# A linear-attention block in one kernel: layernorm applies put ahead of k's exponentials, their statistics a pass sooner, the last v/S tile on two engines

## The chip, the core and the metric

The kernel runs on one core of a Trainium2 chip. The core has TensorE (matrix products, results in PSUM), VectorE, ScalarE (activation functions), GpSimd and SyncE, which here only issues DMAs. In the profile they are PE (and PEld for its weight loads), DVE, ACT, POOL and SP. Each engine works through its own queue in order and waits on semaphores for the others. The metric is the device time of one execution in microseconds (us): a median of 277.12 us in three runs (277.02 to 277.51).

## The reference, cut to what matters

```python
def _A_ref(x, wqkv, w_phi, wo):
    qkv = (x @ wqkv).reshape(B, S, 3, H, Dh)...            # S=2048, D=640, H=32, Dh=20
    q, k, v = qkv[0], qkv[1], qkv[2]
    pq, pk = q @ w_phi, k @ w_phi                          # per head, 20x20
    phi_q = concat([softmax(pq), softmax(-pq)])            # over the 20 features of a head
    phi_k = concat([softmax(pk), softmax(-pk)])
    kv = einsum("bhsf,bhsd->bhfd", phi_k, v)
    z  = einsum("bhsf->bhf", phi_k)
    o = (phi_q @ kv) / (phi_q @ z + 1e-6)
    return o.reshape(B, S, D) @ wo

h  = x + _A_ref(layernorm(x), ...)
h2 = h + (gelu(layernorm(h) @ w_gate) * (layernorm(h) @ w_up)) @ w_down   # F = 1536
```

The softmax of k and its negative gives two "signs", 0 and 1, each with its own sum S over the 20 features of a head. The kernel does not divide the exponentials by S; it divides v by it, which gives the same kv.

## The kernel before, in words

The 2048 rows are 16 tiles of 128 rows. The whole kernel is recorded in a manual schedule: on every engine the instructions run in the order in which the source issues them, and only semaphores hold them.

A first phase makes the layernorms of tiles 0 to 5 and the folded k weights. Then the loop `for t in range(NT)` (L443) runs 16 passes. Pass t does, in source order:

- `k_tile(t)` (L300): TensorE's k product (10 matmuls of 128x320) into a PSUM tile pk, then on ScalarE two exponentials (L305, plus and minus) into E, the numerators of both signs.
- in pass 0 `ln_ap(6)`, made on VectorE; in passes 10 to 14 `fold`, which makes a part of the folded q weights; in pass 15 four q products and their exponentials.
- `kv_tile(i)` (L332) for the tiles that KVG names: the product of E and vt, 20 matmuls for each tile, sign 0 first; tiles 0 and 1 in pass 5, 2 to 5 in pass 9, 6 to 9 in pass 13, the rest at the end.
- in passes 1 to 11 `v_mm(t + 4)`: the v product of a tile four ahead; it reads LN1T, the transposed layernorm of that tile.
- in passes 1 to 9 `ln_ap(t + 6, on_act=True)` (L256): ScalarE writes the layernorm ln of a tile six ahead (L133), from rstd and mr; SP then issues a DMA that transposes it into LN1T (L149).
- `v_ev(t + 4)` (L291): ScalarE copies v from PSUM to vS.
- in even passes up to 6 `ln_st(t + 8, t + 9)` (L252): the layernorm statistics of two tiles. VectorE makes bn_stats and bn_aggr (L109, L113), GpSimd makes ve, rstd and two mr (L121, L122, L127).
- `k_norm(t)` (L308): VectorE sums E (the reduce sk, L312) and takes reciprocals (rs, L316). Then the v/S products (L320): sign 1 of every tile on GpSimd; sign 0 on GpSimd for the tiles in VP, otherwise on VectorE, put off until after the next tile's reduce. Tile 15's sign 0 product follows its reciprocal at once.

In pass 10 VectorE also makes the layernorms of tiles 0 and 1, which the q products of pass 15 read once SP's transposes have landed. SP's queue holds, in this order, the layernorm transposes, loads of the q weights in passes 7 to 10, the transposes of tiles 0 and 1, and in pass 13 the loads of Wg, Wo and Wu.

PSUM tiles of the loop come from a ring (`gtile`): four buffers up to pass 2, three from pass 3 on, where the fourth becomes the accumulator kvp of the kv products. So a k or v product waits until ScalarE has read the tile three allocations earlier.

After the loop, `kv_mask` (L342) brings kvp into the matrix KV, and the rest of the kernel (attention, output projection, the two layers of the feed-forward part) follows from 71 us on.

Of the kernel before, what the change touches and what calls it, by code (L numbers as in the profile page):

```python
# [10 lines left out]
ALU = mybir.AluOpType  # L11
# [6 lines left out]
def kernel(  # L18
# [12 lines left out]
    nc = tc.nc  # L31
    P = 128
    S = 2048
    D = 640
    H = 32
    Dh = 20
    FF = 1536
    NT = S // P
# [5 lines left out]

    H0 = [(P * c) // Dh for c in range(NC)]
    NH = [(P * c + P - 1) // Dh - H0[c] + 1 for c in range(NC)]
    VP = (0, 2, 4, 6, 9, 11)
    KA, QA = (0, 2, 4), (0, 1, 2, 3, 4)
    LQ = (7, 8, 9, 9, 10)
    FQ = (10, 11, 12, 13, 14)  # L50
# [6 lines left out]
    VC = Dh + 1  # L57
# [3 lines left out]
    UH = H // 2  # L61
# [34 lines left out]
    def small(pool, shape, name, bufs=3):  # L96
        return pool.tile(shape, F32, name=name, bufs=bufs)

    def gtile(name):
        return psG.tile([P, 2, 512], F32, name=name, tag="G")  # L100

    def ln_stats(pool, tiles, tag, act=True, between=None, log=False):

        n = len(tiles)
        mv = small(pool, [P, n, nc.vector.BN_AGGR_DIM], "mv" + tag)
        stats = small(pool, [P, n, 2, nc.vector.BN_STATS_DIM], "stats" + tag)
        for j, xt in enumerate(tiles):
            for i in range(2):
                nc.vector.bn_stats(stats[:, j, i, :], xt[:, i * HD:(i + 1) * HD])  # L109
                if between and i == j == 0:  # L110
                    between()
        for j in range(n):
            nc.vector.bn_aggr(mv[:, j, :], stats[:, j])  # L113
        ve = small(pool, [P, n], "ve" + tag)
        rstd = small(pool, [P, n], "rstd" + tag)
        if log:

            nc.scalar.activation(ve, mv[:, :, 1], ACTF.Ln, bias=eps)
            nc.scalar.activation(rstd, ve, ACTF.Exp, scale=-0.5)
        else:  # L120
            nc.gpsimd.tensor_scalar_add(ve, mv[:, :, 1], EPS)  # L121
            nc.gpsimd.tensor_tensor(rstd, ve, nhalf[:, 0:n], op=ALU.pow)  # L122

        mr = small(pool, [P, n], "mr" + tag)
        if act:
            for j in range(n):
                nc.gpsimd.tensor_scalar(mr[:, j:j + 1], mv[:, j, 0:1], rstd[:, j:j + 1], -1.0,  # L127
                                        op0=ALU.mult, op1=ALU.mult)
        return [(xt, mv[:, j, 0:1], rstd[:, j:j + 1], mr[:, j:j + 1]) for j, xt in enumerate(tiles)]
# [11 lines left out]
    def transpose_to(dst, src, on_pe, on_dve=False):  # L141

        if on_pe:
            tp = psG.tile([P, 16, P], BF16, name="tp", tag="G")
            for c in range(NC):
                nc.tensor.transpose(tp[:, c, :], src[:, c * P:(c + 1) * P], ident)
            (nc.vector.tensor_copy if on_dve else nc.scalar.copy)(dst, tp[:, 0:NC, :])  # L147
        else:
            nc.sync.dma_start_transpose(dst, src)  # L149
# [12 lines left out]
    vS = [p1.tile([P, H, VC], BF16, name=f"vS{i}") for i in range(8)]  # L162
# [89 lines left out]
    def ln_st(*tiles, act=True, between=None, log=False):  # L252
        for t, v in zip(tiles, ln_stats(p1, [x_sb[t // 4][:, t % 4, :] for t in tiles], "1", act, between, log)):
            lnp[t] = v

    def ln_ap(t, on_act=False, on_pe=False):  # L256
        ln = (ln_act if on_act else ln_dve)(p1, "1", *lnp[t])
        if on_pe:
            lnp[t] = ln
        else:  # L260
            transpose_to(LN1T[t // 4][:, :, t % 4 * P:(t % 4 + 1) * P], ln, False)
# [8 lines left out]
    def proj(ps, t, W, us=(0, 1), rows=False):  # L270
        for u, c in sorted(((u, c) for u in us for c in range(NC)), key=lambda x: x[::-1] if rows else x):
            nc.tensor.matmul(ps[:, u, 0:HD], lhsT=lnT(t, c), rhs=W[:, c, u * HD:(u + 1) * HD],  # L272
                             start=(c == 0), stop=(c == NC - 1))
# [26 lines left out]
    def k_tile(t):  # L300
        pk = gtile("pk")
        proj(pk, t, Wk2, rows=t == 0)
        Ek[t] = ev.tile([P, 2, D], BF16, name="E", bufs=8)
        for s in range(2):
            nc.scalar.activation(Ek[t][:, s, :].rearrange("p (u f) -> p u f", u=2), pk[:, :, 0:HD],  # L305
                                 ACTF.Exp, scale=((lnp[t][2], nrstd[t]) if t in CT else (1.0, -1.0))[s])

    def k_norm(t):  # L308


        sk = small(p1, [P, 2 * H], "sk")
        nc.vector.reduce_sum(sk, Ek[t].rearrange("p s (h f) -> p (s h) f", f=Dh), axis=AX.X)  # L312
        if t - 1 in todo:
            todo.pop(t - 1)()
        rs = small(p1, [P, 2 * H], "rs")
        nc.vector.reciprocal(rs, sk)  # L316
        Vt[t] = vt = ev.tile([P, 2, H, VC], BF16, name="vt", bufs=8)

        def mult(s, eng):
            eng.tensor_tensor(vt[:, s], vS[t % 8], rs[:, s * H:(s + 1) * H, None].to_broadcast([P, H, VC]), ALU.mult)  # L320

        mult(1, nc.gpsimd)
        if t in VP:
            mult(0, nc.gpsimd)
        elif t == NT - 1:
            mult(0, nc.vector)
        else:
            todo[t] = lambda: mult(0, nc.vector)

# [2 lines left out]
    def kv_tile(t):  # L332

        for s in range(2):
            for c in range(NC):
                for u in range(2):
                    f0, h0 = u * HD + c * 64, u * UH + 3 * c
                    nc.tensor.matmul(kvp[HALF[u], s, c * 4 * VC:(c + 1) * 4 * VC],  # L338
                                     lhsT=Ek[t][:, s, f0:f0 + 64], rhs=Vt[t][:, s, h0:h0 + 4, :],
                                     start=(c == 0 and t == 0), stop=(t == NT - 1), skip_group_check=True)  # L340
# [13 lines left out]
    def q_mm(j, part=(0, 1)):  # L354

        if 0 in part:
            pqs[j] = gtile("pq")
        for i, bc in enumerate(QG[j]):
            if i not in part:
                continue  # L360
            b, c = divmod(bc, NC)
            for kc in range(NC):
                nc.tensor.matmul(pqs[j][:, i, :], lhsT=Wq2[:, kc, c * P:(c + 1) * P], rhs=LN1T[b][:, kc, :],  # L363
                                 start=(kc == 0), stop=(kc == NC - 1))

    def q_exp(j, signs=(0, 1)):
        for s in signs:
            nc.scalar.activation(Eq[j][:, :, s, :], pqs[j][:, 0:len(QG[j])], ACTF.Exp, scale=(1.0, -1.0)[s])  # L368
# [74 lines left out]
    for t in range(NT):  # L443
        if t == T3:
            ps_cm.close()
            psG = ps_cm.enter_context(tc.tile_pool(name="psG", bufs=3, space=PSUM, reuse_waits="tile"))
            psK = ps_cm.enter_context(tc.tile_pool(name="psK", bufs=1, space=PSUM, reuse_waits="tile"))
            kvp = psK.tile([P, 2, 512], F32, name="kvp")
        k_tile(t)
        if t == 0:  # L450
            ln_ap(6)
        if t in FQ:
            fold(WqT, Wq2, True, [i for i, f in enumerate(FQ) if f == t])
        for j in range(len(QT)):
            if t == QT[j]:
                q_mm(j)
                q_exp(j)
        for i in KVG.get(t, ()):
            kv_tile(i)
        if 0 < t < NT - 4:  # L460
            v_mm(t + 4)
        if t > 0 and t + 6 < NT:
            ln_ap(t + 6, on_act=True)
        if 0 < t < NT - 4:
            v_ev(t + 4)
        if t % 2 == 0 and t + 8 < NT:
            ln_st(t + 8, t + 9)
        k_norm(t)
        load_T(WqT, 0, *[i for i, f in enumerate(LQ) if f == t])
        if t == 10:  # L470

            for i in CT:
                ln_ap(i)
        if t == 9:
            nc.gpsimd.memset(KV, 0.0)
            nc.gpsimd.memset(kmask, 1.0)
            for r in HALF:
                nc.gpsimd.affine_select(out=kmask[r], in_=kmask[r], pattern=[[4, NC], [-Dh, 4]],
                                        compare_op=ALU.is_ge, fill=0.0, base=0, channel_multiplier=1)
                nc.gpsimd.affine_select(out=kmask[r], in_=kmask[r], pattern=[[-4, NC], [Dh, 4]],  # L480
                                        compare_op=ALU.is_ge, fill=0.0, base=Dh - 1, channel_multiplier=-1)
            nc.gpsimd.tensor_copy(KV[:, :, 0, :, KC - 1], kmask)
            nc.gpsimd.tensor_copy(KV[:, :, 1, :, 0], kmask)
        if t == 13:
            nc.sync.dma_start(Wg, wg_v)
            nc.sync.dma_start(Wo, wo_v)
            nc.sync.dma_start(Wu, wu_v)
# [338 lines left out]
```

## Time and profile before

| what | value |
|---|---|
| median of 3 runs | 277.12 us (277.02 to 277.51) |
| the profiled execution, its time | 278.27 us |
| its span, first to last instruction | 276.4 us |
| mean granted TensorE clock | 1.000 |
| busy: PE, DVE, ACT, POOL | 271.0, 176.8, 139.2, 97.2 us |
| DVE busy from 20 to 65 us | 4.90 to 5.00 of every 5 us |
| POOL product (L320, 128x672) | 22 times, 1.34 us each |
| DVE product (L320, 128x672) | 10 times, 0.85 to 1.71 us |

A timeline line gives the start and the duration in us from the span's start, the engine, the source line, the operation with its output and inputs, the count of merged instructions, and in brackets the idle time ahead of it with what ended it. Where several instructions are merged the duration reaches from the start of the first to the end of the last. In the list of waits, a line reads: engine and line that waited, engine and line that ended the wait, us in total, how often, the longest. Buffer numbers are left out of the names, so vt is any tile's v/S.

### The profile page before, as it was taken

How to read it: one execution, taken by the hardware profiler on the slowest of the kernel's cores; microseconds unless marked ns; L12 is line 12 of the kernel's file. 1: busy time of each engine (PE TensorE's matmuls, PEld its weight loads, DVE VectorE, ACT ScalarE, POOL GpSimd, SP SyncE). 2: the span in 40 equal slices, each digit the busy share in tenths (PEclk: the TensorE clock that was granted, in tenths of full speed). 3: DMA queues.
4: the chain of work that ended last, by engine and by line, in shares of the span. 5: the costliest groups of instructions: out<-in, count | busy, mean ns of one | idle time of the engine just before them, and what ended most of it. 6: DMA issues, size and time to landing. Idle time of an engine off the chain costs nothing.

```text
span 276.4 us, 5943 instructions
## 1 busy us (share of the span) xinstructions
PE 271.0 (98%) x2348; PEld 173.5 (63%) x2348; DVE 176.8 (64%) x335; ACT 139.2 (50%) x239; POOL 97.2 (35%) x218
## 2 busy tenths in 40 slices
PE   8999999999999999999999999999999999999995
PEld 4676767775455887788764555675555577444574
DVE  6889999999496776576477773346876333322322
ACT  4879897878489856365543255223245410223100
POOL 4238897774302316355303553102165400000000
PEclk9999999999999999999999999999999999999999
DMA  7963436489730021414111133110123111000011
GB/s 208 191 225 71 53 67 102 71 242 392 271 122 0 4 47 26 95 29 97 24 50 47 26 58 62 25 67 9 47 47 71 26 47 50 25 0 0 2 47 47
DMA packets 42235, 21.37 MB, mean 77 GB/s; under 512 B 35040, under 2 KB 40416, under 8 KB 42208
## 3 DMA queue, kind: packets, MB, share of 16 engines
q1 hardware_dynamic: 42208, 21.01, 30.1%
q8 instruction: 18, 0.29, 0.5%
q14 instruction: 9, 0.07, 0.1%
HBM read 10.18 MB, written 2.62 MB: 46 GB/s over the span
## 4 chain that ended last, share of the span: by engine, by line
PE 79%; DMA 5%; SPq 4%; issue 4%; DVE 3%; POOL 1%; ACT 1%; POOLq 0%; DVEq 0%
PE gu L664 38%; PE pd L683 19%; PE po L604 8%; PE pq L363 5%; PE pv L272 3%; PE ab L532 3%; SPq L186 3%; DMA LN1T<-ln 2%; DMA x_sb<-in_A_x_dram 2%; PE pk L272 2%; DMA WqT<-in_A_wqkv_dram 1%; DVE sk L312 1%; PE kvp L338 1%; DVE rs L316 1%; POOL vt L320 1%
## 5 line engine op out<-in xcount | busy, mean ns | idle before, releaser
L667 ACT ACTIVATE g<-gu 128x512 bf16<-128x512 f32 (+1 forms) x60 | 30.7, 512 | 68.6 <-PE gu L664 68.4
L670 DVE TENSOR_TENSOR GT<-gu,g 128x512 bf16<-128x512 f32 (+1 forms) x60 | 34.4, 580 | 47.9 <-PE gu L664 39.3
L664 PE MATMUL gu<-LN2T,Wg 128*128 128x512 bf16 (+1 forms) x300 | 61.8, 337 | 0.0
L664 PE MATMUL gu<-LN2T,Wu 128*128 128x512 bf16 (+1 forms) x300 | 61.8, 336 | 0.0
L683 PE MATMUL pd<-Wd,GT 128*128 128x320 bf16 (+2 forms) x396 | 53.5, 295 | 0.0
L683 PEld LDWEIGHTS <-GT 128*128 128x128 bf16 x396 | 37.9, 98 | 14.7 <-DVE GT L670 0.2
L664 PEld LDWEIGHTS <-Wu 128*128 128x128 bf16 x300 | 29.3, 98 | 22.6
L664 PEld LDWEIGHTS <-Wg 128*128 128x128 bf16 x300 | 28.8, 98 | 21.4
L272 PEld LDWEIGHTS <-LN1T 128*128 128x128 bf16 x290 | 27.7, 98 | 11.4 <-DMA LN1T<-ln 1.2
L686 DVE TENSOR_TENSOR y<-pd,x_sb 128x320 bf16<-128x320 f32 (+2 forms) x29 | 13.9, 480 | 29.0 <-PE pd L683 29.0
L320 POOL TENSOR_TENSOR vt<-vS,rs 128x672 bf16<-128x672 bf16 x22 | 29.1, 1344 | 9.1 <-DVE rs L316 7.4
L604 PE MATMUL po<-Wo,oT 128*128 128x320 bf16 x160 | 24.3, 299 | 0.0
L272 PE MATMUL pk<-Wk,LN1T 128*128 128x320 bf16 x160 | 24.2, 299 | 0.0
L363 PE MATMUL pq<-LN1T,Wq 128*128 128x512 bf16 x100 | 23.1, 379 | 0.0
L312 DVE TENSOR_REDUCE sk<-E 128x64 f32<-128x1280 bf16 x16 | 22.9, 1429 | 0.0
L368 ACT ACTIVATE Eq<-pq 128x1024 bf16<-128x1024 f32 (+1 forms) x26 | 20.0, 829 | 1.7 <-PE pq L363 1.7
L272 PE MATMUL pv<-Wv,LN1T 128*128 128x320 bf16 x130 | 19.8, 299 | 0.5 <-DMA LN1T<-ln 0.4
L604 PEld LDWEIGHTS <-oT 128*128 128x128 bf16 x160 | 15.6, 98 | 7.4 <-ACT oT L147 0.5
L305 ACT ACTIVATE E<-pk 128x640 bf16<-128x640 f32 x28 | 18.2, 705 | 3.9 <-PE pk L272 3.8
L581 DVE TENSOR_TENSOR tt<-AB,w 128x1280 bf16<-128x1280 f32 x12 | 17.9, 1488 | 1.1 <-POOL w L574 0.9
L133 ACT ACTIVATE ln<-x_sb,v,rstd 128x640 bf16<-128x640 bf16 x14 | 12.9, 920 | 10.7 <-POOL v L643 10.3
L363 PEld LDWEIGHTS <-Wq 128*128 128x128 bf16 x100 | 9.4, 98 | 10.0
(110 smaller groups left out, 292.9 us busy)
## 6 DMA issues: line engine op xcount, KB each, us to landing
out_dram<-y SPq DMA_DIRECT2D x15, 160.0 KB, 1.8
Wg<-in_B_w_gate_dram SPq DMA_DIRECT2D x1, 1920.0 KB, 7.7
Wu<-in_B_w_up_dram SPq DMA_DIRECT2D x1, 1920.0 KB, 13.6
Wd<-in_B_w_down_dram SPq DMA_DIRECT2D x1, 1920.0 KB, 7.8
x_sb<-in_A_x_dram SPq DMA_DIRECT2D x2, 640.0 KB, 7.0
Wo<-in_A_wo_dram SPq DMA_DIRECT2D x1, 800.0 KB, 9.3
x_sb<-in_A_x_dram SPq DMA_DIRECT2D x4, 160.0 KB, 3.2
Wv<-in_A_wqkv_dram SPq DMA_DIRECT2D x2, 320.0 KB, 4.2
```

The source lines that it names most:

```text
L272: nc.tensor.matmul(ps[:, u, 0:HD], lhsT=lnT(t, c), rhs=W[:, c, u * HD:(u + 1) * HD], start=(c == 0), stop=(c == NC - 1))
L305: nc.scalar.activation(Ek[t][:, s, :].rearrange("p (u f) -> p u f", u=2), pk[:, :, 0:HD], ACTF.Exp, scale=((lnp[t][2], nrstd[t]) if t in C ...
L312: nc.vector.reduce_sum(sk, Ek[t].rearrange("p s (h f) -> p (s h) f", f=Dh), axis=AX.X)
L320: eng.tensor_tensor(vt[:, s], vS[t % 8], rs[:, s * H:(s + 1) * H, None].to_broadcast([P, H, VC]), ALU.mult)
L363: nc.tensor.matmul(pqs[j][:, i, :], lhsT=Wq2[:, kc, c * P:(c + 1) * P], rhs=LN1T[b][:, kc, :], start=(kc == 0), stop=(kc == NC - 1))
L368: nc.scalar.activation(Eq[j][:, :, s, :], pqs[j][:, 0:len(QG[j])], ACTF.Exp, scale=(1.0, -1.0)[s])
L581: nc.vector.tensor_tensor(tt.rearrange("p s (h f) -> p s h f", f=Dh), num, w[:, :, :, None].to_broadcast([P, 2, H, Dh]), ALU.mult)
L604: nc.tensor.matmul(pos[u], lhsT=st[t][:, c, :], rhs=Wo[:, c, u * HD:(u + 1) * HD], start=(c == 0), stop=(c == NC - 1))
L664: nc.tensor.matmul(gu[i][:, 0:n], lhsT=W[:, c, f * P:(f + 1) * P], rhs=LN2T[b][:, c, a0:a1], start=(c == 0), stop=(c == NC - 1))
L667: nc.scalar.activation(g[:, 0:n], gu[0][:, 0:n], ACTF.Gelu_apprx_tanh)
L670: nc.vector.tensor_tensor(st[b, "g", f][:, a0:a1], gu[1][:, 0:n], g[:, 0:n], ALU.mult)
L683: nc.tensor.matmul(ps, lhsT=st[b, "g", f][:, tl * P:(tl + 1) * P], rhs=Wd[:, f, f0:f1], start=(f == 0), stop=(f == NF - 1))
```

## The change

Three edits in the loop, and one in `k_norm`:

- From pass 2 on, the layernorm apply of tile t+6 stands ahead of `k_tile(t)`, so ahead of k's exponentials on ScalarE; in pass 1 it stays where it was.
- The statistics of tiles 10 to 15, in pairs, move from passes 2, 4 and 6 to passes 1, 3 and 5.
- Tile 13's sign 0 product goes to GpSimd (VP gets 13).
- Tile 15's sign 1 product is cut by heads: the first 16 on GpSimd, the other 16 on VectorE, behind VectorE's sign 0 product.

TensorE's and SP's instructions keep their order.

```diff
-    VP = (0, 2, 4, 6, 9, 11)
+    VP = (0, 2, 4, 6, 9, 11, 13)
...
-        def mult(s, eng):
-            eng.tensor_tensor(vt[:, s], vS[t % 8], rs[:, s * H:(s + 1) * H, None].to_broadcast([P, H, VC]), ALU.mult)
-
-        mult(1, nc.gpsimd)
+        def mult(s, eng, a=0, b=H):
+            eng.tensor_tensor(vt[:, s, a:b], vS[t % 8][:, a:b],
+                              rs[:, s * H + a:s * H + b, None].to_broadcast([P, b - a, VC]), ALU.mult)
+
+        mult(1, nc.gpsimd, 0, UH if t == NT - 1 else H)
         if t in VP:
             mult(0, nc.gpsimd)
         elif t == NT - 1:
             mult(0, nc.vector)
+            mult(1, nc.vector, UH)
         else:
             todo[t] = lambda: mult(0, nc.vector)
...
+        if t > 1 and t + 6 < NT:
+            ln_ap(t + 6, on_act=True)
         k_tile(t)
...
-        if t > 0 and t + 6 < NT:
-            ln_ap(t + 6, on_act=True)
+        if t == 1:
+            ln_ap(7, on_act=True)
         if 0 < t < NT - 4:
             v_ev(t + 4)
-        if t % 2 == 0 and t + 8 < NT:
-            ln_st(t + 8, t + 9)
+        if t == 0 or t % 2 and t + 9 < NT:
+            ln_st(t + 9 - (t == 0), t + 10 - (t == 0))
         k_norm(t)
```

## The prediction

> **What bounds the kernel now.** I read the page first (engine table and the sums of the chain), then what TensorE waited for, then the timelines of TensorE, VectorE and GpSimd between 20 and 72 us, the only stretch that the change touches.
>
> ```profile
> span 276.4 us, 5943 instructions
> PE 271.0 (98%) x2348; PEld 173.5 (63%) x2348; DVE 176.8 (64%) x335; ACT 139.2 (50%) x239; POOL 97.2 (35%) x218
> ...
> PE 79%; DMA 5%; SPq 4%; issue 4%; DVE 3%; POOL 1%; ACT 1%; POOLq 0%; DVEq 0%
> ```
>
> TensorE is busy 98% of the span, so the change can only win what TensorE waits for, but can lose whatever it makes TensorE wait. The waits:
>
> ```profile
> PE kvp L338 <- POOL vt L320: 0.5, 1, 0.5
> ...
> PE pv L272 <- DMA LN1T<-ln: 0.4, 1, 0.4
> ```
>
> The first is the last v/S tile (70.17 to 70.72). The second lies at 22.24, on tile 6, whose path is not changed. A third shows only as a gap in TensorE's timeline: by its 1.36 us step the v product of tile 12 should start at 39.91 and starts at 40.20, and the chain leads there through a late layernorm of tile 12. So 0.55 + 0.29 = 0.84 us is the most there is to win.
>
> ```profile
> 38.55 1.52 PE L272 MATMUL pk<-Wk,LN1T 128*128 128x320 bf16 x10
> 40.20 1.53 PE L272 MATMUL pv<-Wv,LN1T 128*128 128x320 bf16 x10
> ...
> 60.24 7.72 PE L363 MATMUL pq<-LN1T,Wq 128*128 128x512 bf16 x35
> 67.89 2.29 PE L338 MATMUL kvp<-vt,E 128*64 128x84 bf16 x110
> 70.72 0.38 PE L338 MATMUL kvp<-vt,E 128*64 128x84 bf16 x10 [0.55 <-POOL vt L320]
> 71.04 2.33 PE L363 MATMUL pq<-LN1T,Wq 128*128 128x512 bf16 x10
> ```
>
> The engine behind these waits is VectorE. In the windows from 20 to 65 us it is busy 4.90 to 5.00 of every 5 us: any time added to its queue there stays in it until the last v/S tile. The layernorms of tiles 0 and 1, which it makes in pass 10, also gate q: the second transpose is issued at 55.56 and, the slower of the two, takes 4.2 us to land (2.6/3.4/4.2 min/median/max), so at 59.8, 0.4 us before q starts at 60.24. That is all the slack it has.
>
> Now how VectorE and GpSimd meet:
>
> ```profile
> 25.13 2.59 POOL L320 TENSOR_TENSOR vt<-vS,rs 128x672 bf16<-128x672 bf16 x2
> 27.81 0.23 POOL L121 TENSOR_SCALAR ve<-mv 128x2 f32<-128x2 f32 x1
> 28.12 0.71 POOL L122 TENSOR_TENSOR rstd<-ve,nhalf 128x2 f32<-128x2 f32 x1
> 28.93 0.96 POOL L127 TENSOR_SCALAR mr<-mv,rstd 128x1 f32<-128x1 f32 x2
> ...
> 27.32 1.43 DVE L312 TENSOR_REDUCE sk<-E 128x64 f32<-128x1280 bf16 x1
> 28.67 0.85 DVE L320 TENSOR_TENSOR vt<-vS,rs 128x672 bf16<-128x672 bf16 x1
> 29.44 0.55 DVE L316 RECIPROCAL rs<-sk 128x64 f32<-128x64 f32 x1
> ...
> 44.03 2.59 POOL L320 TENSOR_TENSOR vt<-vS,rs 128x672 bf16<-128x672 bf16 x2
> ...
> 45.94 1.40 DVE L320 TENSOR_TENSOR vt<-vS,rs 128x672 bf16<-128x672 bf16 x1
> ```
>
> At 28.67 VectorE's product of tile 1 (sign 0) meets only GpSimd's small statistics and takes 0.85. At 45.94 the same instruction finds a GpSimd product running until 46.62 and ends at 47.34, 0.72 after it: it was held. The one at 55.86 takes 1.71 against a GpSimd product that started 0.32 earlier (55.54) and ended at 56.85: again the end plus 0.72. Whoever starts first keeps the other out, and a lead of 0.32 us is enough. In the last pair VectorE starts 0.07 first (68.64 against 68.71), and GpSimd's product takes 1.97 for 1.31.
>
> **The change, part by part.**
>
> *Statistics a pass sooner.* The pairs (10,11), (12,13) and (14,15) move from behind the even reduce to ahead of the odd one. VectorE's work is the same; what moves is the GpSimd queue. There the four statistics instructions now stand between the two products of an even tile and the one of the odd tile. Before, they stood behind it, exactly where VectorE's own product of the odd tile fell. Now the odd tile's GpSimd product falls there:
>
> Tile 1: GpSimd's second product ends at 25.13 + 1.31 = 26.45. The statistics took 27.72 to 29.89 = 2.17, of which the mr pair was held 0.46 (0.96 against 0.50 at 22.98), so 1.71. Product from 26.45 + 1.71 + 0.09 = 28.25 to 29.56. VectorE reaches its product at 28.67 as before (the same work stands ahead of it, in another order). GpSimd leads by 0.42, so VectorE ends at 29.56 + 0.72 = 30.28 for 29.52: +0.75.
>
> Tile 3: the reciprocal of tile 2 now starts at 30.20. GpSimd: 30.75 + 0.22 to start + 2.59 + 1.80 = 35.35, ends 36.66. VectorE: 2.23 (reciprocal and statistics) + 1.53 + 0.47 + 1.35 later, 35.78. Held to 37.38 for 36.63: +0.75.
>
> Tile 5, by the same steps: GpSimd 42.39 to 43.70, VectorE at 42.88, held to 44.42 for 43.73: +0.69.
>
> Sum: VectorE is 2.2 us late from pass 6 on. Bounds of each hold: 0 (VectorE first; then the GpSimd product waits 0.7, which has slack) and 1.3 (a whole product). I take the worked 0.7 because the lead (0.4) lies above the 0.32 that the trace shows to decide.
>
> The Trainium skill ("SBUF — State Buffer", section "SBUF: two separate sides") speaks against such a meeting: the two engines share a port pair under an exclusive lock, and the loser waits out the whole instruction. The rows differ in detail: 0.72 of the 0.85 is still to do after a hold, and the product at 28.67 was not held by the small rstd running until 28.83. By the page's rule taken to the letter, each hold costs 0.13 more, 0.4 in sum.
>
> *Applies ahead of k's exponentials.* Nothing is added; ScalarE makes ln(t+6) 0.92 sooner and E(t) as much later. E is needed by the reduce, which runs at least 1.5 us behind (48.90 to 50.38 in pass 10, over 2 us in passes 2 to 9), and by the PSUM ring of three: v of tile 7 may wait 0.1 for E of tile 2. ln(14) now stands ahead of E of tile 8 and waits for its mr at about 42.1; E of tile 8 then ends near 44.3, not 41.4, and its reduce (now 46.8) still waits for nothing. The copy of v of tile t+8 writes the vS that the held products read, so it now also waits for them: tile 11's, at about 38.7 on ScalarE, needs tile 3's product (37.4), tile 13's, at 46, needs tile 5's (44.4); both are in time. The transposes keep their order on SP. ln(12) gets its mr before 35.0, not at 35.8, so its transpose lands at about 39.2 and the 0.29 at 39.91 goes. But the products of tiles 2 to 5 (from 42.7, twenty matmuls in 0.41) reach tile 5 at 43.97 and wait for 44.42: -0.29 + 0.51 on TensorE.
>
> *What is late next.* The layernorms of tiles 0 and 1 come 2.2 us later, the second lands at 59.81 + 2.2 = 62.0, and SP's Wg, Wo, Wu behind it slide as much (Wo is first read at 80.27, landed by 69). q starts at 62.05 for 60.24: +1.81. TensorE, there at about 60.5, hides its own 0.2 in this wait.
>
> *Tile 13 to GpSimd, last tile shared.* Tile 13's sign 0 product leaves VectorE (0.91) and costs GpSimd 1.31. Reciprocal 13 at 64.90. GpSimd: tile 13 both signs 65.6 to 68.2, tile 14 to 69.45. VectorE: reduce 14 at 65.37, reduce 15 at 67.37, product 14 at 68.72, held to 70.17. So the 0.91 comes back as a hold. Last reciprocal 70.09 to 70.64; VectorE's sign 0 to 71.59; GpSimd's half (half of the 1.17 that it took after VectorE's end: 0.59) to 72.18; VectorE's half after it (half of 0.72) to 72.5. q follows 0.37 after the tile as before: 72.9 for 71.04, +1.85. If VectorE takes its half first, GpSimd's ends at 72.6.
>
> The skill ("GPSIMD Engine Reference", "Engine selection") advises VectorE for elementwise work, GpSimd being about 2x slower on two inputs; the rows say 1.31 to 0.85, 1.5x. By 2x, tile 14 would end 0.4 later and so would the sum.
>
> **Sum.** Both gates agree: q +1.81, last tile +1.85. Behind 71 us TensorE has no slack to give back (50.0 of 50 us busy from 90 to 140), so +1.85 reaches the end. The profiled execution took 278.27 (span 276.4), 1.15 above the median of 277.12; I carry the difference to the median: 278.97, so 279.0, +0.67%.
>
> **Rivals.**
> - *No holds* (VectorE takes the port first, or the GpSimd statistics run 0.4 slower): it decides where GpSimd's lead falls under zero; the rows leave 0.07 to 0.32 open. The 0.29 is won; at the end GpSimd's tile 13 (64.70 to 65.97) and 14 (to 67.24) hold VectorE's product 14 to 67.96 for 68.07, and the shared last tile ends at 70.3 for 70.67: -0.37, 276.75. At most all 0.84: 276.3. For it: 0.1 us of semaphore time would eat a quarter of the lead. Against: the lead is 0.42, 0.43 and 0.49 in the three places.
> - *Some holds only*: one leaves 59.81 + 0.75, q +0.37 and the last tile -0.37 + 0.75: 277.5. Two: +1.1, 278.2.
> - *More than worked*: the second transpose already takes 4.2 for the first's 2.6, with the weights' traffic on its heels; if GpSimd or a landing costs another 1 us there, 280.0.
> - *Hidden*: VectorE late, but TensorE not. Against: 0.4 us of slack at q, none at the last tile.
>
> **Chances.** Forecast 0.66 (its own range 278.4 to 279.6), no holds 0.14, some 0.11, more 0.09. The measurement tells about 0.2% (0.55 us) from no change. Slower: 0.66 + 0.09 + 0.08 of the some = 0.83. Same: 0.03 of the some and 0.08 of no holds = 0.11. Faster: 0.06. The range drops most of "no holds" and the worst of "more": 277.2 to 279.9.
>
> **What would show it.** VectorE's sign 0 products of tiles 1, 3 and 5 at about 1.6 us instead of 0.85; the reciprocal of tile 6 near 44.3; a TensorE wait at the first q for LN1T of about 1.5 us; the gap ahead of tile 12's v product gone; tile 14's product on VectorE held behind GpSimd. I am wrong if those products stay at 0.85.

## The result, and the profile after

The change makes the kernel slower: 278.51 us median (278.08 to 279.31, 6 runs) for 277.38 (277.02 to 277.51), a ratio of 1.0041 with a 95% interval of 1.0029 to 1.0053. Beside the last experiments, on another chip, it was measured again: 1.0037 (1.0023 to 1.0050). So +1.0 to +1.1 us, where +1.85 was forecast. The profiled execution of the changed kernel took 278.30 us, span 276.6.

First the page of the changed kernel, the engine line and the chain that ended last:

```profile
PE 270.0 (98%) x2335; PEld 173.4 (63%) x2348; DVE 179.2 (65%) x335; ACT 138.6 (50%) x239; POOL 96.3 (35%) x219
...
PE 72%; DVE 17%; issue 6%; DMA 1%; ACT 1%; POOL 1%; SPq 0%; DVEq 0%; ACTq 0%
```

VectorE has 2.4 us more of busy time (179.2 for 176.8), although a product of 0.91 us left it and only half a product came to it. Its share of the chain went from 3% to 17% (7% in the later profile of the change, for 4% in that of before): the loop's end now hangs more on its queue. Where it was held, in the timelines of GpSimd, VectorE and TensorE of the changed kernel:

```profile
22.73 2.58 POOL L320 TENSOR_TENSOR vt<-vS,rs 128x672 bf16<-128x672 bf16 x2 [0.38 <-ACT vS L292]
25.41 0.23 POOL L121 TENSOR_SCALAR ve<-mv 128x2 f32<-128x2 f32 x1
25.72 0.71 POOL L122 TENSOR_TENSOR rstd<-ve,nhalf 128x2 f32<-128x2 f32 x1
26.53 0.50 POOL L127 TENSOR_SCALAR mr<-mv,rstd 128x1 f32<-128x1 f32 x2
26.98 1.31 POOL L320 TENSOR_TENSOR vt<-vS,rs 128x672 bf16<-128x672 bf16 x1
...
33.93 1.31 POOL L320 TENSOR_TENSOR vt<-vS,rs 128x672 bf16<-128x672 bf16 x1
...
40.74 1.31 POOL L320 TENSOR_TENSOR vt<-vS,rs 128x672 bf16<-128x672 bf16 x1
...
69.14 1.40 POOL L320 TENSOR_TENSOR vt<-vS,rs 128x336 bf16<-128x336 bf16 x1 [1.35 <-DVE rs L316]
...
26.20 1.43 DVE L312 TENSOR_REDUCE sk<-E 128x64 f32<-128x1280 bf16 x1
27.55 1.47 DVE L320 TENSOR_TENSOR vt<-vS,rs 128x672 bf16<-128x672 bf16 x1
...
34.51 1.45 DVE L320 TENSOR_TENSOR vt<-vS,rs 128x672 bf16<-128x672 bf16 x1
...
41.46 1.31 DVE L320 TENSOR_TENSOR vt<-vS,rs 128x672 bf16<-128x672 bf16 x1
...
67.05 1.46 DVE L320 TENSOR_TENSOR vt<-vS,rs 128x672 bf16<-128x672 bf16 x1
...
69.07 1.83 DVE L320 TENSOR_TENSOR vt<-vS,rs 128x672 bf16<-128x672 bf16 x2
...
60.20 7.71 PE L365 MATMUL pq<-LN1T,Wq 128*128 128x512 bf16 x34 [0.56 <-DMA LN1T<-ln]
...
70.59 0.20 PE L340 MATMUL kvp<-vt,E 128*64 128x84 bf16 x1 [0.22 <-POOL vt L320]
70.95 0.35 PE L340 MATMUL kvp<-vt,E 128*64 128x84 bf16 x9 [0.17 <-DVE vt L320]
```

VectorE's products of tiles 1, 3 and 5 take 1.47, 1.45 and 1.31 us; before, each took 0.85. The first starts at 27.55 while GpSimd's product runs from 26.98 to 28.29, and ends 0.73 after it; the other two end 0.72 after GpSimd's products of 33.93 and 40.74. The three holds add 0.62 + 0.60 + 0.46 = 1.68 us. TensorE waits for the layernorm of tile 1 at the first q product (0.56) and for both halves of the last tile; the wait at tile 12's v product is gone.

The two profiled executions did not start the loop at the same time. The timeline of VectorE before, then after; the first line of each is the statistics of tile 6, the first instruction that needs the load of x for tiles 6 and 7:

```profile
17.40 0.89 DVE L109 BATCH_NORM_STATS2 stats<-x_sb 128x6 f32<-128x320 bf16 x2 [1.11 <-DMA x_sb<-in_A_x_dram]
...
21.69 1.43 DVE L312 TENSOR_REDUCE sk<-E 128x64 f32<-128x1280 bf16 x1
```

```profile
16.28 0.88 DVE L109 BATCH_NORM_STATS2 stats<-x_sb 128x6 f32<-128x320 bf16 x2
...
20.56 1.43 DVE L312 TENSOR_REDUCE sk<-E 128x64 f32<-128x1280 bf16 x1
```

In the one of before VectorE waited 1.11 us for this load, in the other not at all, and its first reduce moved with it. That is why the two spans (276.4, 276.6) seem to hide the loss. I therefore read every kernel by the time from this first reduce to the end of the last kv matmul, called the *loop time* below: before 70.72 + 0.38 - 21.69 = 49.41 us, after 70.95 + 0.35 - 20.56 = 50.74, so +1.33. From there to the end of the span it is 205.3 us in both (276.4 - 71.1, 276.6 - 71.3): nothing is given back or lost later.

### The profile page after: what moved, and what is told of

Read it like the earlier page. It is cut to its first block, busy times and chain, and to the rows that moved or that the text cites. A ratio compares the mean times of both kernels' runs of the same rounds, so it can differ in the third digit from the quotient of the medians.

```text
span 276.6 us, 5929 instructions
## 1 busy us (share of the span) xinstructions
PE 270.0 (98%) x2335; PEld 173.4 (63%) x2348; DVE 179.2 (65%) x335; ACT 138.6 (50%) x239; POOL 96.3 (35%) x219
## 2 busy tenths in 40 slices
DMA packets 42235, 21.37 MB, mean 77 GB/s; under 512 B 35040, under 2 KB 40416, under 8 KB 42208
## 4 chain that ended last, share of the span: by engine, by line
PE 72%; DVE 17%; issue 6%; DMA 1%; ACT 1%; POOL 1%; SPq 0%; DVEq 0%; ACTq 0%
PE gu L668 37%; PE pd L687 19%; PE po L608 8%; DVE sk L312 6%; PE pq L365 5%; DVE stats L109 4%; DVE rs L316 3%; PE ab L536 2%; DMA x_sb<-in_A_x_dram 1%; DVE vt L320 1%; DVE ln L138 1%; DVE mv L113 1%; PE tp L146 0%; ACT L671 0%; DVE LN1T L147 0%
## 5 line engine op out<-in xcount | busy, mean ns | idle before, releaser
L320 POOL TENSOR_TENSOR vt<-vS,rs 128x672 bf16<-128x672 bf16 (+1 forms) x23 | 29.9, 1318 | 11.0 <-DVE rs L316 7.9
```

The lines of the kernel that those rows point to most:

```text
L320: eng.tensor_tensor(vt[:, s, a:b], vS[t % 8][:, a:b], rs[:, s * H + a:s * H + b, None].to_broadcast([P, b - a, VC]), ALU.mult)
```

## The experiments

Theory A: the loss is the three holds, made by GpSimd's order. Theory B: ScalarE's order, the applies ahead of the exponentials. Theory C: tile 13 on GpSimd and the shared last tile. Theory D, formed later: VectorE's early statistics cost something whatever they meet.

| kernel | ratio to before (95%) | loop time, us | first reduce, us |
|---|---|---|---|
| before; again in a later run | 1 | 49.41; 49.4 | 21.69; 21.26 |
| the change; again | 1.0041 (1.0029-1.0053); 1.0037 (1.0023-1.0050) | 50.74; 50.8 | 20.56; 20.43 |
| statistics sooner alone | 1.0060 (1.0044-1.0075) | 51.1 | 21.33 |
| change, applies put back | 1.0033 (1.0021-1.0046) | 50.7 | 21.04 |
| tail alone | 0.9989 (0.9977-1.0001) | 49.1 | 21.15 |
| last tile shared alone | 0.9991 (0.9980-1.0002) | 49.2 | 21.37 |
| applies alone | 1.0002 (0.9991-1.0014) | 49.4 | 21.79 |
| change, GpSimd's order put back | 1.0035 (1.0021-1.0049) | 50.6 | 20.77 |
| the same, applies put back | 1.0002 (0.9992-1.0013) | 49.6 | 20.96 |
| change, odd products at once | 1.0017 (1.0005-1.0030) | 50.2 | 20.59 |
| the same, tile 14 last | 1.0008 (0.9995-1.0020) | 49.5 | 21.29 |
| tail, tile 14 last | 0.9987 (0.9977-0.9998) | 48.7 | 21.09 |

**Statistics a pass sooner, alone**, on the kernel before:

```diff
-        if t % 2 == 0 and t + 8 < NT:
-            ln_st(t + 8, t + 9)
+        if t == 0 or t % 2 and t + 9 < NT:
+            ln_st(t + 9 - (t == 0), t + 10 - (t == 0))
```

> The kernel before with one edit: the statistics a pass sooner (applies, tile 13 and the last tile as before). Theory A (GpSimd's four statistics instructions push its odd product onto VectorE's, which is held): VectorE's products of tiles 1, 3, 5 take 1.3 to 1.5 us as in the changed kernel (0.85 before), VectorE is about 1.7 us late, and the time is 1.1 to 1.7 us above before, ratio 1.004 to 1.006. Theory B (ScalarE's late exponentials and the PSUM ring): within 0.3 us of before, ratio 0.999 to 1.001. Theory C (tile 13 on GpSimd and the shared last tile): the same as before.

Slower by 0.60%, 1.7 us, and the loop time is 1.7 up: by loop time more than the whole change (51.1 for 50.74), while the intervals of the two ratios overlap. Its VectorE products (instructions on vt, durations in ns min/median/max) and TensorE's waits:

```profile
L320 DVE TENSOR_TENSOR vt<-vS,rs x10: 859/1344/1716, 28.3 to 70.0; 128x672 bf16<-128x672 bf16 x10
...
PE kvp L338 <- POOL vt L320: 0.8, 1, 0.8
PE kvp L338 <- DVE vt L320: 0.7, 1, 0.7
```

Half of the ten products now take over 1.34 us (918 ns median before), and TensorE waits 1.5 us for the last two v/S tiles. Theories B and C can't give this: neither edit is in it.

**The change with the applies put back** behind the exponentials, all else changed:

```diff
-        if t > 1 and t + 6 < NT:
-            ln_ap(t + 6, on_act=True)
         k_tile(t)
...
-        if t == 1:
-            ln_ap(7, on_act=True)
+        if t > 0 and t + 6 < NT:
+            ln_ap(t + 6, on_act=True)
```

> The changed kernel with the applies put back behind the exponentials (statistics a pass sooner, tile 13 and the last tile as in the change). Theory A: still slower by 0.9 to 1.4 us, ratio 1.003 to 1.005, with the three held products. Theory B: the loss is gone, ratio 0.998 to 1.001. Theory C: as slow as the change, but without need of held products.

1.0033, and the three products at 1.47, 1.45 and 1.30: theory B is out as the cause.

**The tail alone**, on the kernel before (`mult` takes a range of heads, as in the change):

```diff
-    VP = (0, 2, 4, 6, 9, 11)
+    VP = (0, 2, 4, 6, 9, 11, 13)
...
-        mult(1, nc.gpsimd)
+        mult(1, nc.gpsimd, 0, UH if t == NT - 1 else H)
...
             mult(0, nc.vector)
+            mult(1, nc.vector, UH)
```

> The kernel before with the tail's edits alone: tile 13's sign 0 product on GpSimd and the last tile's sign 1 cut between the two engines. Theory A: nothing lost, -0.4 to +0.1 us, ratio 0.9985 to 1.0005, because the 0.9 us off VectorE comes back as a hold of its tile 14 product. Theory B: the same as before. Theory C: slower by about 1.1 us, ratio 1.004.

0.9989: no loss, rather a small gain whose interval just reaches 1. VectorE's product of tile 14 took 1.45 for 0.93, the hold that theory A named. Theory C is out.

**The change with GpSimd's order put back.** VectorE's part of the statistics stays early; GpSimd's four instructions are issued behind the odd product:

```diff
+            late = [] if t % 2 else None
-            ln_st(t + 9 - (t == 0), t + 10 - (t == 0))
+            ln_st(t + 9 - (t == 0), t + 10 - (t == 0), late=late)
         k_norm(t)
+        if t % 2 and t + 9 < NT:
+            late.pop()()
```

(`late` collects what L121 to L127 do, for the call behind `k_norm`.)

> The changed kernel with one thing put back: on GpSimd alone the four statistics instructions of passes 1, 3 and 5 stand behind the odd tile's product again; VectorE's, ScalarE's, TensorE's and SP's orders are those of the change. Theory A: the three VectorE products fall to 0.85 to 1.0 us, VectorE is on time, and the loss is gone: -0.5 to +0.3 us against before, ratio 0.998 to 1.001. Theories B and C: still slower by about 1.1 us, ratio 1.004.

A miss: 1.0035, though the holds were all but gone. GpSimd's, VectorE's, ScalarE's and TensorE's timelines of this kernel:

```profile
26.64 1.31 POOL L325 TENSOR_TENSOR vt<-vS,rs 128x672 bf16<-128x672 bf16 x1 [1.11 <-DVE rs L321]
...
27.75 0.91 DVE L325 TENSOR_TENSOR vt<-vS,rs 128x672 bf16<-128x672 bf16 x1
...
29.94 0.92 ACT L138 ACTIVATE ln<-x_sb,mr,rstd 128x640 bf16<-128x640 bf16 x1 [2.27 <-POOL mr L128]
30.77 1.27 ACT L310 ACTIVATE E<-pk 128x640 bf16<-128x640 f32 x2
...
32.10 1.52 PE L277 MATMUL pv<-Wv,LN1T 128*128 128x320 bf16 x10 [0.91 <-ACT E L310]
...
38.48 0.70 PE L277 MATMUL pv<-Wv,LN1T 128*128 128x320 bf16 x4 [0.79 <-ACT E L310]
```

The product takes 0.91: GpSimd's ended 0.20 us into it (27.95), so only 0.06 was left to wait. But with GpSimd's statistics later, mr is later; the apply, now ahead of the exponentials, waits 2.27 us for it, E of tile 4 stands behind it, and with E the PSUM buffer that tile 9's v product needs. TensorE waits 0.91, and again 0.79 at tile 11: 1.7 us in its list of waits. Another loss of the same size had taken the place of the first.

**The same with the applies put back** tells whether that was all:

```diff
-        if t > 1 and t + 6 < NT:
-            ln_ap(t + 6, on_act=True)
         k_tile(t)
...
-        if t == 1:
-            ln_ap(7, on_act=True)
+        if t > 0 and t + 6 < NT:
+            ln_ap(t + 6, on_act=True)
```

> The changed kernel with two things put back: on GpSimd the statistics of passes 1, 3 and 5 behind the odd product, and the applies behind k's exponentials. VectorE still makes its statistics a pass sooner; tile 13 and the last tile are as in the change. Theory A (held products are the loss; the run before this one lost its time instead on exponentials queued behind an apply that waited for a late mr): products of tiles 1, 3, 5 at 0.85 to 0.95 us, no wait of a v product for E, -0.5 to +0.2 us against before, ratio 0.998 to 1.0007. Theory D (VectorE's early statistics cost something by themselves, or tile 13 does): still 1.003 to 1.004.

1.0002, the products at 0.91, no wait for E. TensorE's one wait in the loop is 0.6 us ahead of tile 12's v product, whose layernorm is late with mr; at the last tile it no longer waits, and the loop time is 0.2 up. The statistics are early on VectorE and tile 13 is on GpSimd, so theory D is out too: what costs is what GpSimd's order makes wait, VectorE in the one queue order, ScalarE in the other.

**The applies alone**, on the kernel before:

```diff
+        if t > 1 and t + 6 < NT:
+            ln_ap(t + 6, on_act=True)
         k_tile(t)
...
-        if t > 0 and t + 6 < NT:
-            ln_ap(t + 6, on_act=True)
+        if t == 1:
+            ln_ap(7, on_act=True)
```

> The kernel before with the applies ahead of k's exponentials and nothing else. Theory A: VectorE's products of tiles 1, 3, 5 stay at 0.85; but mr comes as late as before, the applies of tiles 10, 12 and 14 wait for it with E of tiles 4, 6 and 8 queued behind, and the v products of tiles 9, 11 and 13 wait for E, longest at tile 11 (0.8 to 1.0 us); part of it is paid back by the waits that before has at tile 12 and at the end, so +0.2 to +0.8 us, ratio 1.0005 to 1.003. Theory B (ScalarE's order is free): no wait for E, ratio 0.998 to 1.000.

1.0002 (0.9991 to 1.0014), below the expected 1.0005 to 1.003. The mechanism is there, but in one place (tile 11) where three were expected, one wait of a v product for E:

```profile
PE pv L272 <- ACT E L305: 0.7, 1, 0.7
```

Its price is not, or less than can be told: TensorE's wait for the last tile, 0.5 before, is not in its list any more, and the loop time is the same (49.4). Here the wait in mid-loop took the place of a wait at the end.

**The last tile shared, alone**; tile 13 stays on VectorE:

```diff
-        mult(1, nc.gpsimd)
+        mult(1, nc.gpsimd, 0, UH if t == NT - 1 else H)
...
             mult(0, nc.vector)
+            mult(1, nc.vector, UH)
```

> The kernel before with the last tile's sign 1 product cut between GpSimd and VectorE, tile 13 as before. Theory A: the last tile is complete 0.2 us sooner after its reciprocal (1.83 for 2.03 us), so -0.3 to 0.0 us, ratio 0.9988 to 1.0.

0.9991 (0.9980 to 1.0002), loop time 0.2 down: as expected in size, and not told apart from no change.

**The kernel before again**, not edited, one profile.

> The kernel before again, one look. Theory A together with the reading that the first profiled execution started VectorE's loop late (x landed late): VectorE's first reduce of the loop at 20.5 to 21.4 us, not 21.69, the wait for the last v/S tile 0 to 0.4 us, not 0.55, and a span of 275.3 to 276.0. If the start does not vary between executions, 21.7 and 0.55 come again.

First reduce at 21.26 and span 276.0, so the start does vary; but the wait for the last tile was 0.5 again, against the expectation. TensorE had started as much earlier as VectorE (first q product at 59.82 for 60.24), so their distance was unchanged: 49.4 us of loop time both times.

**The change with the odd products at once.** The same instructions and the same GpSimd and ScalarE queues, but VectorE's products of tiles 1, 3 and 5 follow their own reciprocals, where GpSimd is at its small statistics:

```diff
             todo[t] = lambda: mult(0, nc.vector)
+            if t in (1, 3, 5):
+                todo.pop(t)()
```

> The changed kernel, with VectorE's products of tiles 1, 3 and 5 made at once behind their own reciprocal instead of behind the next reduce: the same instructions and the same GpSimd and ScalarE queues, but the products now fall on GpSimd's four small statistics instructions and not on its product. Theory A: those three products take 0.85 to 0.95 us, the 1.7 us of holds is gone; a reciprocal that has nothing between it and its reduce costs 0.2 us each, so VectorE is 0.5 to 0.6 us late at tile 7; no v product waits for E. -0.4 to +0.3 us against before, ratio 0.9985 to 1.001. Theory D (the loss comes with VectorE's early statistics or ScalarE's order, whatever meets whom): 1.003 to 1.004 as in the change.

GpSimd, then VectorE:

```profile
25.75 0.72 POOL L122 TENSOR_TENSOR rstd<-ve,nhalf 128x2 f32<-128x2 f32 x1
26.57 1.00 POOL L127 TENSOR_SCALAR mr<-mv,rstd 128x1 f32<-128x1 f32 x2
27.54 1.31 POOL L320 TENSOR_TENSOR vt<-vS,rs 128x672 bf16<-128x672 bf16 x1
...
25.76 0.55 DVE L316 RECIPROCAL rs<-sk 128x64 f32<-128x64 f32 x1
26.35 0.86 DVE L320 TENSOR_TENSOR vt<-vS,rs 128x672 bf16<-128x672 bf16 x1
27.12 1.48 DVE L312 TENSOR_REDUCE sk<-E 128x64 f32<-128x1280 bf16 x1
28.64 0.55 DVE L316 RECIPROCAL rs<-sk 128x64 f32<-128x64 f32 x1
```

0.86 us each: moved away from GpSimd's product, none is held; GpSimd's mr pair is, to 1.00 from 0.50. The ratio is 1.0017, over the 1.001 expected. From one reciprocal to the next it is 28.64 - 25.76 = 2.88 us, against 2.65 with the product behind the reduce and GpSimd's order put back (25.94 to 28.59), and 0.36 and 0.30 more at the other two tiles: a product that waits for the reciprocal just ahead of it, and a reciprocal right behind its reduce, cost more than the 0.2 that I took; VectorE is 1.1 us late by tile 8, not 0.6. The hold and its absence are shown; this kernel is no cure.

**Tile 14's product behind the last reciprocal**, once on the last kernel (e_now in what was expected) and once on the tail alone:

```diff
-        if t - 1 in todo:
+        if t - 1 in todo and t < NT - 1:
             todo.pop(t - 1)()
         rs = small(p1, [P, 2 * H], "rs")
         nc.vector.reciprocal(rs, sk)
+        if t - 1 in todo:
+            todo.pop(t - 1)()
```

> The run e_now with one more move: in the last pass VectorE's product of tile 14 stands behind the last reciprocal instead of ahead of it, when GpSimd is through with tile 14. Theory A: that product falls from 1.46 to about 0.9 us, the last reciprocal ends 1.4 us sooner, the last v/S tile makes TensorE wait no more: 0.2 to 0.5 us below e_now, ratio to before 0.997 to 1.000.

> The kernel before with tile 13 on GpSimd, the last tile shared, and VectorE's product of tile 14 behind the last reciprocal; statistics and applies as before. Theory A: no wait for the last v/S tile (0.7 us in the kernel before), the 0.3 ahead of tile 12's v product stays: -0.8 to -0.3 us, ratio 0.997 to 0.999.

1.0008 (0.9995 to 1.0020) and 0.9987 (0.9977 to 0.9998). The first is 0.3 us below the kernel it was made from, as expected, but over its expected 1.000: TensorE waits no more for the last tile, but 0.7 us for a layernorm at the first q product. The second is faster than the kernel before by 0.13%, or 0.4 us, in the ratio, though the two medians differ by only 0.1 us (277.30 for 277.43). The largest gain, in a kernel without the three new holds, is this small because TensorE is busy 98% anyway. Its VectorE and TensorE at the end:

```profile
66.11 0.55 DVE L316 RECIPROCAL rs<-sk 128x64 f32<-128x64 f32 x1
66.58 2.54 DVE L322 TENSOR_TENSOR vt<-vS,rs 128x672 bf16<-128x672 bf16 x3
...
59.69 7.72 PE L367 MATMUL pq<-LN1T,Wq 128*128 128x512 bf16 x35
67.34 2.48 PE L342 MATMUL kvp<-vt,E 128*64 128x84 bf16 x120
69.75 1.47 PE L367 MATMUL pq<-LN1T,Wq 128*128 128x512 bf16 x6
```

All 120 kv matmuls run in one piece: the last tile is ready at 69.12, ahead of its turn.

**The change again**, not edited, beside these.

> The changed kernel again, beside the others on one chip. Theory A: 1.003 to 1.005, VectorE's product of tile 15 starts 48.5 us after its first reduce of the loop (46.95 before), whatever time that reduce starts at.

1.0037; the product of tile 15 starts at 68.98, 48.55 us after a first reduce at 20.43, as expected from the first profile.

## Why the prediction was right, and where its numbers were off

- *TensorE's waits are all there is to win, 0.84 us*: right as a bound. The best kernel won 0.4 by the ratio, 0.1 between the medians, 0.7 in loop time.
- *GpSimd's odd product falls onto VectorE's and holds it, three times*: right, shown by the three durations, by the statistics moved alone (1.0060) and by the products moved away (0.86 each). The no-holds rival is out; GpSimd led in all three places.
- *The size of the holds, 0.75 + 0.75 + 0.69 = 2.2*: too big; 0.62 + 0.60 + 0.46 = 1.68. The term that failed is GpSimd's start, "1.71 + 0.09" after its second product. It was 26.98 - 25.31 = 1.67, not 1.80: the product starts 0.05 before the mr pair's end (26.53 + 0.50), where I put a gap of 0.09. GpSimd led by 0.57, 0.58 and 0.72, not by 0.42, 0.43 and 0.49, so VectorE had less of GpSimd's product left to wait out. (At tile 5, 0.08 of the difference is VectorE's own, which came that much later than worked out.) The rule that the forecast used, GpSimd's end plus 0.72, held; a larger lead means a shorter hold.
- *The kv products wait 0.51 for tile 5* (the two times given there, 43.97 and 44.42, are 0.45 apart): didn't come. Tile 5's product ended at 42.77 and TensorE reached tile 5 no earlier than 43.5 (42.26 and three tiles of 0.41). The forecast took both engines' starts from the profile of before; in that of the change VectorE began 1.13 sooner (20.56 for 21.69), TensorE's kv products only 0.5 sooner than worked out.
- *Tile 12's wait goes*: right, no gap there after.
- *q waits about 1.5 us*: 0.56 in one profile of the change. In the other it is 0.3, put down to ScalarE's last cast of the q weights (L236, until 59.59) and not to LN1T, and the end waited longer (0.9 us in all, for 0.4). The two gates share the loss, and which one shows it varies.
- *The tail*: right in detail. Tile 14's product took 1.46 (1.45 worked out), the last tile 1.83 from VectorE's start (1.76 worked out; 2.03 before). So tile 13's product gains on VectorE's queue almost only what the hold takes back, and sharing the last tile wins 0.2.
- *The applies ahead add nothing*: right in the change, where mr comes early. The prediction didn't say that the two edits need each other: with mr at its old time, the apply holds the exponentials and TensorE behind them.
- *The sum, +1.85*: in loop time +1.33 and +1.4, in the medians +1.1 and +1.0, so 278.51 lies at the lower end of the forecast's own range (278.4 to 279.6). Of the 0.5 between forecast and loop time, the holds' 0.5 is all. The rest, 0.2 to 0.4, lies inside the ratio's interval (0.8 to 1.5 us) and stays open. Both profiles of before started late (spans of 276.4 and 276.0, where the 82 runs of before beside the experiments have a median of 275.5), so no profile shows its loop time after an early start.

The Trainium skill's exclusive port pair ("SBUF — State Buffer", section "SBUF: two separate sides") describes what the runs show, one engine waiting for the other's instruction; the three holds ended 0.72 to 0.73 after GpSimd's product, where waiting out the instruction and then starting afresh would be 0.85. The same number fits every VectorE product that started during a GpSimd product in these two profiles, six before and eight after: each ended 0.71 to 0.73 after GpSimd's. So the products of 0.91 and 0.93 us were held a little too, and such a product's end can be worked out ahead as the later of its own start plus 0.85 and GpSimd's end plus 0.72. The prediction's reading that the small rstd did not hold the product at 28.67 is not shown: rstd's end plus 0.72 is 29.55, and the product ended at 29.52, which both readings allow.

## What to carry to other kernels

Before a step is moved in one engine's queue, look at what then falls beside it on an engine whose instructions the rows show it waiting for: in the kernel with the statistics alone the work of every engine stayed the same, and three meetings of two products cost 1.7 us. A queue that is busy all the time, VectorE's here, has no slack, so each meeting adds up until the next hard gate; a mid-loop wait on an engine that waits at the gate anyway can cost nothing, as 0.7 us for 0.5 did here. Compare profiles from a common event inside the kernel, not from the span's start, when the first loads land at different times.

## What was not expected

- The start of the loop varies by execution with the landing of the x load for tiles 6 and 7: VectorE's first reduce lay between 20.43 and 21.79 us in the fourteen profiled executions, 21.26 and 21.69 for the one kernel of before. It lay at 20.43 to 20.59 in the three that did not wait for that load, and later in all that did. The loop time behind it repeats within 0.1 us (49.41 and 49.4; 50.74 and 50.8). Between the two profiles of before it moved the span by 0.4 us (276.4 and 276.0). Its whole range, 1.4 us, is as much as the change, but no one kernel was seen across it.
- Who is held depends on who starts first, to a few hundredths: at 69.07 VectorE began 0.07 before GpSimd (69.14), took 0.86 as if alone, and GpSimd's half tile took 1.40. GpSimd's mr pair, which starts behind a VectorE product, is held by it (1.00 for 0.50). Whether a small GpSimd instruction holds VectorE in turn is not shown: the product at 26.35 started before rstd's end (26.47) and ended at 27.21, which is near both 26.47 + 0.72 and 26.35 + 0.85.
